# The last stage of an FNet and GEGLU kernel: two row tiles move from plain products into the seven-product scheme, and SiLU is taken per row tile

## The chip, the cores and the metric

The kernel runs on one core of a Trainium2 chip. The metric is the device time of one execution in microseconds; the time before is 771.11 us, the median of three runs (770.98 to 771.66). One further execution was taken by the hardware profiler; all durations of single instructions come from it.

## The reference

The input x has 2048 rows of 448 features, float32. What is computed:

```
xn = layernorm(x)
a, b = xn @ dft_hid_re.T, xn @ dft_hid_im.T          # DFT over the features
s    = dft_seq_re @ a - dft_seq_im @ b               # real part of the DFT over the rows
g    = silu((gelu(xn @ w_gate) * (xn @ w_up)) @ w_down)
out  = x + s * g
```

The two DFTs over the rows are products of a 2048x2048 and a 2048x448 matrix each. They are the last stage, and the change is in it.

## The kernel before

Every float32 operand is split into a high part of reduced precision, which TensorE takes in one pass, and a low part (the rest). A product is then high by high, and high by low, and low by high.

The stages follow each other: layernorm and transposes of x; gate, up and down of the GEGLU, with g summed into a DRAM tensor `gs`; the **hidden stage**, which computes a and b for 16 row tiles k of 128 rows (`hid_mm`, 22 products each); and the **last stage**, about 285 us long, which this case is about.

In the last stage the 16 output row tiles are done in eight pairs. For a pair j the sum over k runs over 16 **units**. For 14 row tiles k a unit is the function `seven`: a Strassen-like scheme with seven products in place of eight, each two matmuls (128x448 and 128x224), into seven PSUM banks that gather over the units. For the two row tiles in `KP` (10 and 15) a unit, called t0 and t1, is the function `plain`: twelve matmuls of 128x448 for one output row tile, into a bank of its own.

Each unit needs coefficients. `load_c` brings raw columns of the DFT matrix (`ct`, 192 KB, on SP's queue) and sums that were made earlier in DRAM (`sums`, 128 KB, on POOL's queue) into one of five raw buffers; a plain unit needs `cp` alone (256 KB). `sum_c` adds two more sums on VectorE (lines 1051 and 1052). `prep_c` splits the raw buffer: the high part on ScalarE (line 142), the low part on VectorE (line 143), into one of four slots that go round, and then asks for the load of five units on into the raw buffer just read. While TensorE works on unit m, the program's order has VectorE do `sum_c(m + 4)` and then `prep_c(m + 3)`. A slot is free for the high part of unit m + 3 when TensorE is done with unit m - 1.

The split values of a row tile k, seven blocks of 448 columns, lie in SBUF (`TS`). There isn't room for all: two tiles of the set `KX` are in SBUF at a time, the other two in DRAM (`td`), and each pair loads two of them on ScalarE's queue (line 1287, four loads for each tile, at the units named in `LOAD_AT`). The order of the row tiles alternates, so that a pair begins with the tiles with which the last one ended.

At a pair's end `gather` adds the seven banks into the two output tiles: one copy on ScalarE (line 1247) and seven operations of VectorE (lines 1249 to 1255). After that come one addition for each tile's halves, the addition of the plain bank (1309, 1316), the product with g (1262), the addition of x by a DMA (1264) and the store; five of these VectorE operations are handed out one to a unit in the next pair. SiLU of g was taken in the hidden stage, on four chunks of 1792 columns, read from `gs` and written back (line 1101). The last pair has an order of its own (`last_pair`).

The order on every engine is written out by hand: the program's text is the order of each engine's queue, and semaphores carry the waits between them.

Of the kernel before, what the change touches and what calls it, by code (L numbers as in the profile page):

```python
# [45 lines left out]
def fnet_geglu(ctx: ExitStack, tc: tile.TileContext, x, ca, ct, cp, et, wgu, wd, out):  # L46
# [496 lines left out]
    with tc.manual_schedule():  # L543
# [231 lines left out]
        sums = [dram.tile([P, NS, 2 * P], F32, name=f"sums{j}") for j in range(NK // 2)]  # L775

        def sum_step(at):


            for d in (0, 2):  # L780
# [3 lines left out]
                for n in (slice(0, NS // 2), slice(NS // 2, NS)):  # L784
# [124 lines left out]

        td = {k: dram.tile([P, 7 * D], F32, name=f"td{k}") for k in KX[0] + KX[1]}  # L910
        new = {}

        def place(tag, n):
# [11 lines left out]
            4: lambda: vt[1],  # L925
            5: lambda: slot(1),
            6: lambda: slot(0),
            7: lambda: a_x[1],
            8: lambda: a_h[0],
            9: lambda: a_h[1],  # L930
            11: lambda: a_x[2],
            12: lambda: place("st", 8 * D),
            13: lambda: place("x0", 4096),
            14: lambda: a_x[3],
        }
# [10 lines left out]
        def f_at(k):  # L946
            return (a_t if k % 2 == 0 or k > 12 else a_r[0])[:, : 8 * HD]

        TS, ab, ab_at, behind = {}, {}, {}, []
# [19 lines left out]
        def hid_plain(k, ps, spots):  # L969
            ab_at[k] = spots  # L970
# [6 lines left out]
            ab[k] = [(v[:, :D], v[:, D:]) for v in spots]  # L977
# [19 lines left out]
        def hid_split(k):  # L997

            f = fs[k].rearrange("p (i d) -> p i d", d=HD)[:, :7]
            TS[k] = AT[k]()[:, :T7]  # L1000
# [12 lines left out]
        units = [(j, k) for j in range(NK // 2) for k in order(j) + ["t0", "t1"]]  # L1013
        UN = NS + 2

        def raw_at(m):
            if m in (4, 5, 9, 10):
                return cc[:, 896 * ((m + 1) % 5) :][:, :896]
            i = (2, 0, 1, 2, 0, 0, 0, 1, 2)[m] if m < 9 else (m - 11) % 5
# [3 lines left out]
        nxt = {0: 3, 1: 6, 2: 7, 3: 8, 9: None, 10: None}  # L1023
# [9 lines left out]
        def load_c(m):  # L1033
# [7 lines left out]
            if isinstance(k, str):  # L1041
                nc.sync.dma_start(v[:, : 4 * P], cp[2 * j + int(k[1])])
            else:
                nc.sync.dma_start(v[:, : 3 * P], ct[j, :, KS.index(k)])
                nc.gpsimd.dma_start(v[:, 4 * P : 6 * P], sums[j][:, KS.index(k)])  # L1045
# [22 lines left out]
        g_in = {}  # L1068
        for k in [*range(14), 15, 14]:
# [6 lines left out]
            if k == 13:  # L1076
                behind.pop(0)()
# [8 lines left out]
            if k not in KP:  # L1086
                behind.append(lambda k=k: hid_split(k)())
                if k == 13:
                    behind.pop()()
# [3 lines left out]
            if k == 4:  # L1093
                x0 = sb.tile([P, 4096], F32, name="g_in", tag="x0")
            for c, at, v in ((2, 3, (a_st, 0)), (3, 4, None), (0, 4, None), (1, 5, (a_st, 1))):
                if k == at:
                    v, i = v or (x0, int(c == 0))
                    g_in[c] = part(v, 4 * D * i, 4, D)
                    nc.sync.dma_start(g_in[c], gv[:, 4 * c : 4 * c + 4])
                if k == at + 3:  # L1100
                    nc.scalar.activation(g_in[c], g_in[c], AF.Silu)
                    nc.sync.dma_start(gv[:, 4 * c : 4 * c + 4], g_in[c])
# [6 lines left out]
            if k == 12:  # L1109
                load_c(1)  # L1110
                load_c(2)
            if k == 13:
                sum_c(3)
        cc = sb.tile([P, 4 * D], F32, name="cc", tag="d1")
        load_c(4)
        load_c(5)
# [7 lines left out]
        gx = [v[:, o : o + D].bitcast(F32) for v, o in ((E_IN[2], 4 * D), (new["st"], T7))]  # L1124
# [12 lines left out]
        LOAD_AT = 2, 3, 4, 5, 6, 7, 8, 9  # L1137
        LAST_AT = 2, 2, 3, 4, 5, 6, 7, 8
# [6 lines left out]

        def seven(m, ps, n=1, only=None):

            for q, (i, b) in PRODUCTS.items():
                if only and q not in only:
                    continue  # L1150
                for u in range(m, m + n):
                    v = TS[units[u][1]][:, b * D : (b + 1) * D]
# [6 lines left out]
                        start=False, stop=u % UN == NS - 1, skip_group_check=True,  # L1159
                    )  # L1160

        def plain(m, py):
            h, l = c_hl.pop(m)
            for i, k in enumerate(KP):
                for r in range(2):
                    vh, vl = ab[k][r]
                    o = (2 * i + r) * P
                    a, b = h[:, o : o + P], l[:, o : o + P]
                    nc.tensor.matmul(py[:, :D], a, vh, start=i + r == 0, stop=False)  # L1169
                    nc.tensor.matmul(py[:, :D], a, vl, start=False, stop=False)  # L1170
# [219 lines left out]
```

## Time and profile before

| quantity | value |
|---|---|
| median of three runs | 771.11 us |
| time of the profiled execution | 771.12 us |
| span of the profiled execution, first to last instruction | 769.0 us |
| TensorE busy / VectorE / ScalarE / GpSimd | 99% / 71% / 48% / 23% |
| granted TensorE clock | 1.00 |
| DMA moved | 170.04 MB, mean 221 GB/s |

PE is TensorE's matmul, PEld its weight load, DVE VectorE, ACT ScalarE, POOL GpSimd and SP the sync engine, which only issues DMAs. A matmul's duration is longer than the distance to the next one's start, since matmuls are pipelined; the distance is what counts. So it is with VectorE: an operation on 128x896 is shown with 1.08 us, and the next begins 1.00 us after its start. The DMA share can exceed 1 where packets overlap.

### The profile page before, as it was taken

What the parts mean: (1) busy time and instruction counts of PE and PEld (TensorE: products, weight loads), DVE (VectorE), ACT (ScalarE), POOL (GpSimd) and SP (SyncE); (2) the same over time, 40 slices, a digit from 0 to 9 for tenths busy, and PEclk for the clock granted to TensorE, in tenths of its full rate; (3) what the DMA queues carried; (4) which work ended last, traced back from release to release, by engine and by line L of the source; (5) the groups of instructions that cost most, each with busy time, mean ns of one, the idle gap of its engine ahead of it and who ended that gap; (6) DMA issues with size and microseconds to landing.
All of it is one profiled execution on the core that took longest, in us unless ns stands there. A gap on an engine that the chain in (4) does not pass through costs nothing.

```text
span 769.0 us, 11358 instructions
## 1 busy us (share of the span) xinstructions
PE 763.1 (99%) x4056; PEld 687.5 (89%) x4056; DVE 544.8 (71%) x948; ACT 365.4 (48%) x545; POOL 177.5 (23%) x300
## 2 busy tenths in 40 slices
PE   9999999999999999999999999999999999999997
PEld 8988888888888888888889999999999999999997
DVE  7889877555556556455452776888888797979787
ACT  4875554444444344344444585544444444434341
POOL 1204033330511511501011001223232222313130
PEclk9999999999999999999999999999999999999999
DMA  8234458994959968774989981959696969788794
GB/s 295 92 119 145 150 202 171 263 185 102 264 111 248 272 116 227 169 158 84 258 217 242 370 343 55 315 177 340 203 355 205 349 206 334 219 295 266 255 310 155
DMA packets 61369, 170.04 MB, mean 221 GB/s; under 512 B 7424, under 2 KB 40064, under 8 KB 60416
## 3 DMA queue, kind: packets, MB, share of 16 engines
q0 software_dynamic: 13728, 61.02, 34.9%
q1 hardware_dynamic: 34128, 82.48, 30.5%
q10 hardware_dynamic: 13456, 25.81, 9.2%
q8 instruction: 32, 0.52, 0.3%
q14 instruction: 25, 0.20, 0.1%
HBM read 127.21 MB, written 70.91 MB: 258 GB/s over the span
## 4 chain that ended last, share of the span: by engine, by line
PE 96%; DVE 3%; ACT 1%; issue 0%; DVEq 0%; ACTq 0%
PE x L465 24%; PE p L1154 22%; PE po L442 18%; PE p L1157 10%; PE ab L965 9%; PE x L472 4%; PE gu L388 3%; PE py L1169 1%; PE py L1171 1%; PE py L1170 1%; PE warm L565 1%; DVE st L155 1%; PE p L1187 0%; PE pt L198 0%; DVE xt L215 0%; DVE xr_a L189 0%
## 5 line engine op out<-in xcount | busy, mean ns | idle before, releaser
L465 PE MATMUL x<-xt,w 128*128 128x512 f32 x480 | 149.5, 392 | 0.0
L465 PEld LDWEIGHTS x<-xt,w 128*128 128x128 f32 x480 | 90.1, 188 | 16.4 <-DVE tmp L504 0.7
L449 ACT ACTIVATE po_out<-po 128x448 f32<-128x448 f32 x112 | 60.1, 537 | 81.6 <-PE po L442 79.2
L442 PE MATMUL po<-wd0h,hs 128*128 128x448 f32 x256 | 81.7, 366 | 0.1
L454 POOL DMA_DIRECT2D gs<-po_out x24 | 21.4, 890 | 218.8 <-ACT po_out L449 213.6
L965 PE MATMUL ab<-e,xt 128*128 128x448 f32 x288 | 68.8, 365 | 0.0
L442 PE MATMUL po<-wd,hs 128*128 128x448 f32 x288 | 66.0, 365 | 0.0
L465 PE MATMUL x<-t_v,w 128*128 128x512 f32 x216 | 60.7, 389 | 0.0
L442 PEld LDWEIGHTS po<-wd,hs 128*128 128x128 f32 x288 | 54.1, 188 | 6.7
L965 PEld LDWEIGHTS ab<-e,xt 128*128 128x128 f32 x288 | 54.1, 188 | 4.3
L442 PEld LDWEIGHTS po<-wd0h,hs 128*128 128x128 f32 x256 | 48.1, 188 | 5.2 <-DVE tmp L416 0.3
L465 PEld LDWEIGHTS x<-t_v,w 128*128 128x128 f32 x216 | 40.5, 188 | 8.7
L1045 POOL DMA_DIRECT2D raw<-sums x45 | 24.8, 551 | 96.5 <-DVE xt L143 58.5
L442 PE MATMUL po<-wd0l,hs 128*128 128x448 f32 x128 | 46.9, 366 | 0.0
L142 ACT ACTIVATE e<-raw 128x896 fp32r<-128x896 f32 (+1 forms) x30 | 27.7, 922 | 39.0 <-DVE raw L1052 26.1
L520 ACT ACTIVATE hs<-tmp 128x512 fp32r<-128x512 f32 x24 | 15.2, 634 | 54.5 <-DVE tmp L518 54.5
L465 PE MATMUL x<-t_lo,w 128*128 128x512 f32 x96 | 37.4, 389 | 0.0
L142 ACT ACTIVATE e<-tmp 128x896 fp32r<-128x896 f32 (+1 forms) x22 | 19.7, 897 | 36.3 <-DVE tmp L1052 26.8
L1154 PE MATMUL p<-t_v,wd0l 128*128 128x448 f32 x112 | 36.4, 374 | 0.0
L1154 PE MATMUL p<-w,e 128*128 128x448 f32 x112 | 36.4, 374 | 0.0
L1045 POOL DMA_DIRECT2D tmp<-sums x39 | 21.4, 550 | 61.1 <-DVE xt L143 44.5
L350 DVE TENSOR_TENSOR w<-raw,w 128x512 fp32r<-128x512 f32 (+1 forms) x24 | 21.3, 888 | 18.3 <-ACT w L348 18.3
(369 smaller groups left out, 2016.8 us busy)
## 6 DMA issues: line engine op xcount, KB each, us to landing
gs<-po_out POOLq DMA_DIRECT2D x24, 896.0 KB, 8.5
sums<-ca SPq DMA_DIRECT2D x16, 896.0 KB, 10.0
sums<-ca POOLq DMA_DIRECT2D x16, 896.0 KB, 14.6
t_v<-td ACTq DMA_DIRECT2D x24, 448.0 KB, 5.8
w<-td ACTq DMA_DIRECT2D x24, 448.0 KB, 7.3
raw<-ct SPq DMA_DIRECT2D x45, 192.0 KB, 4.2
raw<-wgu SPq DMA_DIRECT2D x12, 640.0 KB, 5.9
tmp<-ct SPq DMA_DIRECT2D x39, 192.0 KB, 4.6
```

The lines of the kernel that those rows point to most:

```text
L142: nc.scalar.activation(h, src, AF.Copy)
L350: nc.vector.tensor_sub(w[:, 1408 + lo : 1408 + b], raw[:, P + lo : P + b], hw[:, lo:b].bitcast(F32))
L388: nc.tensor.matmul(ps[:, cols], a, xt[:, cols], start=n == 0, stop=n == len(mm) - 1)
L442: nc.tensor.matmul(po[:, :D], hs[:, a, kk * P : (kk + 1) * P], wdn[b][:, i], start=n == 0, stop=n == 5,)
L449: nc.scalar.activation(out_[0][:, kk], po[:, :D], AF.Copy)
L454: nc.gpsimd.dma_start(gv[:, 4 * c : 4 * c + 4], out_[0], accum_op=ALU.add)
L465: nc.tensor.matmul(ps, a[i], b[j], start=first and n == 0, stop=n == 2, skip_group_check=True)
L472: nc.tensor.matmul(ps, a[0], xt, start=False, stop=True, skip_group_check=True)
L965: nc.tensor.matmul(p[:, :D], a, b, start=n == 0, stop=n == len(mm) - 1)
L1045: nc.gpsimd.dma_start(v[:, 4 * P : 6 * P], sums[j][:, KS.index(k)])
L1154: nc.tensor.matmul(ps[q][:, :D], h, v, start=u % UN == 0, stop=False, skip_group_check=True)
L1157: nc.tensor.matmul(ps[q][:, :HD], l, v[:, :HD], start=False, stop=u % UN == NS - 1, skip_group_check=True,)
```

## The change

All 16 row tiles go through `seven` in the first seven pairs; the plain units t0 and t1 are left to the last pair alone, whose plain row tiles are now 8 and 10. The set `KX` has three tiles on each side, so that six lie in DRAM and each pair loads three, in twelve loads at the units 1 to 11. The last two units of a pair are done together: for each product, the matmuls of both units, then the next product. So the banks are complete one after another, while the pair still runs, and `gather` follows at that place. The banks go round by one, so that the next pair begins on the one bank that is not waited for. The values of row tile 13 lie in four pieces (`wide`), in what was the room of the plain tiles.

SiLU on the four chunks is gone from the hidden stage, with its loads and stores. In its place ScalarE takes SiLU of one 128x448 tile after each tile's first addition (`sum_` in `give`), in place in the half of `cc` that this addition has just read, and the product with g reads it there.

```diff
-KR = (2, 3, 6, 7, 8, 9, 11, 12, 13, 14)
-KX = ((4, 5), (0, 1))
-KP = (10, 15)
-KS = sorted(KR + KX[0] + KX[1])
-NS = len(KS)
+KR = (3, 4, 6, 7, 9, 11, 12, 13, 15, 14)
+KX = ((5, 8, 10), (0, 1, 2))
+KP = KX[0][1:]
+KW = 13
+LAST = NK // 2 - 1
+NL = NK - len(KP)
 def order(j):
-    return [*KX[j % 2], *KR, *KX[(j + 1) % 2]]
+    k = [*KX[j % 2], *KR, *KX[(j + 1) % 2]]
+    return k if j < LAST else k[:NL] + ["t0", "t1"]
...
-        sums = [dram.tile([P, NS, 2 * P], F32, name=f"sums{j}") for j in range(NK // 2)]
+        sums = [dram.tile([P, NK, 2 * P], F32, name=f"sums{j}") for j in range(NK // 2)]
...
+        pd = {k: dram.tile([P, 4 * D], F32, name=f"pd{k}") for k in KP}
...
-            if k in KP:
-                hid_plain(k, ps, [rest(v) for v in ((vt[0], t_lo[0]), (place("x0", 4096), a_x[2]) if k > 10 else None)[k > 10]])
-            else:
-                hid_sums(k, ps)()
+            hid_sums(k, ps)()
+            if k in KP:
+                hid_plain(k, ps)
...
-                if k == at + 3:
-                    nc.scalar.activation(g_in[c], g_in[c], AF.Silu)
-                    nc.sync.dma_start(gv[:, 4 * c : 4 * c + 4], g_in[c])
+            if k == 5:
+                nc.scalar.activation(tbl, epst, AF.Silu)
...
-        LOAD_AT = 2, 3, 4, 5, 6, 7, 8, 9
-        LAST_AT = 2, 2, 3, 4, 5, 6, 7, 8
+        LOAD_AT = 1, 2, 3, 4, 5, 5, 6, 7, 8, 9, 10, 11
+        LAST_AT = 1, 2, 3, 4, 5, 5, 6, 7
...
         def give(j, t):
             c = cs[t][0]
             def out_():
-                nc.vector.tensor_mul(c, c, gx[t])
+                nc.vector.tensor_mul(c, c, cs[t][1])
                 nc.gpsimd.dma_start(c, xv[:, 2 * j + t, :D], accum_op=ALU.add)
                 stores.append(lambda: nc.sync.dma_start(ov[:, 2 * j + t], c))
-            return [lambda: nc.vector.tensor_add(c, c, cs[t][1]), out_]
+            def sum_():
+                nc.vector.tensor_add(c, c, cs[t][1])
+                nc.scalar.activation(cs[t][1], gx[t], AF.Silu)
+            return [sum_, out_]
...
+            if u < (NL - 2 if j == LAST else UN - 2):
+                seven(m, ps)
+            elif j < LAST and u == UN - 2:
+                seven(m, ps, 2)
...
+            if m:
                 sum_c(m + 4)
                 prep_c(m + 3)
+            if u == UN - 2:
+                todo = gather(ps)
+                for f in todo[:6]:
+                    f()
+            if u == UN - 1:
+                todo[6]()
+                spare = give(j, 0) + give(j, 1)
+                banks = banks[7:] + banks[:7]
+                continue
+            if m == 2:
+                behind.pop()()
...
+                sums14()
             if m == 6:
                 hid_split(14)()
```

The change moves instructions on VectorE at the pair's end. Before, there stand in a row, from the first of the seven gathering operations of the second pair (`p_1` are its banks, `cc` the output tiles; `xt_67` and `wd0l`, then `e_3019`, `e_2921` are the slots of the units):

```order
L1249 TENSOR_TENSOR cc<-cc,p_1_4179 128x2x224
L1250 TENSOR_TENSOR cc<-cc,p_1_4180 128x2x224
L1251 TENSOR_TENSOR cc<-cc,p_1_4181 128x2x224
L1051 TENSOR_TENSOR raw_d_3414<-raw_d_3414 128x128
L1052 TENSOR_TENSOR raw_d_3414<-raw_d_3414 128x128
L143 TENSOR_TENSOR xt_67<-raw_74,wd0l 128x896
L1252 TENSOR_TENSOR cc<-cc,p_1_4182 128x2x224
L1253 TENSOR_TENSOR cc<-p_1_4182,cc 128x2x224
L1254 TENSOR_TENSOR cc<-cc,p_1_4183 128x2x224
L1255 TENSOR_TENSOR cc<-p_1_4184,cc 128x2x224
L1309 TENSOR_TENSOR cc<-cc,py_1_4481 128x448
L1051 TENSOR_TENSOR tmp<-tmp 128x128
```

And now, at the same place of the changed program:

```order
L1263 TENSOR_TENSOR cc<-cc,p_1_4209 128x2x224
L1264 TENSOR_TENSOR cc<-cc,p_1_4210 128x2x224
L1265 TENSOR_TENSOR cc<-cc,p_1_4211 128x2x224
L1266 TENSOR_TENSOR cc<-cc,p_1_4212 128x2x224
L1267 TENSOR_TENSOR cc<-p_1_4212,cc 128x2x224
L1268 TENSOR_TENSOR cc<-cc,p_1_4213 128x2x224
L1082 TENSOR_TENSOR tmp<-tmp 128x128
L1083 TENSOR_TENSOR tmp<-tmp 128x128
L145 TENSOR_TENSOR e_2921<-tmp,e_2921 128x896
L1269 TENSOR_TENSOR cc<-p_1_4214,cc 128x2x224
L1082 TENSOR_TENSOR raw_74<-raw_74 128x128
L1083 TENSOR_TENSOR raw_74<-raw_74 128x128
```

Six of the seven now stand together, ahead of the sums and the low part of the third unit to come, and the addition of a plain bank is gone.

On ScalarE, before, from the copy of the first bank of the same pair on (`td` are the kept tiles' loads):

```order
L1247 ACTIVATE cc<-p_1_4178 128x2x224
L142 ACTIVATE wd0l<-raw_74 128x896
L142 ACTIVATE e_3019<-raw_d_3414 128x896
L142 ACTIVATE e_2921<-tmp 128x896
L142 ACTIVATE t_v_820<-tmp 128x896
L142 ACTIVATE wd0l<-raw_74 128x896
L1287 DMA t_v_820<-td_3214 128x2x448
L142 ACTIVATE e_3019<-raw_74 128x896
L1287 DMA t_v_820<-td_3214 128x896
```

And in the changed program:

```order
L1261 ACTIVATE cc<-p_1_4208 128x2x224
L144 ACTIVATE e_2921<-tmp 128x896
L144 ACTIVATE t_v_820<-tmp 128x896
L1284 ACTIVATE cc<-e_3019 128x448
L1299 DMA t_v_820<-td_3215 128x2x448
L144 ACTIVATE wd0l<-raw_74 128x896
L1299 DMA t_v_820<-td_3215 128x896
L144 ACTIVATE e_3019<-raw_74 128x896
L1284 ACTIVATE cc<-ts_st 128x448
L1299 DMA t_v_820<-td_3215 128x2x448
```

The rows of line 1284 are SiLU. Each stands ahead of a high part and of a kept tile's load, and behind it in the queue wait the high parts of all later units.

More of the change, by code (lines that the diff above doesn't have):

```diff
@@ L999, in hid_split, with low @@
             f = fs[k].rearrange("p (i d) -> p i d", d=HD)[:, :7]
+            if k == KW:
+                for i, v in enumerate((vt[0], t_lo[0], place("x0", 4096), a_x[2])):
+                    w = min(2, 7 - 2 * i)
+                    wide.append(rest(v))
+                    v = wide[i][:, : w * D].rearrange("p (i w d) -> p i w d", i=w, w=2)
+                    nc.scalar.activation(v[:, :, 0], f[:, 2 * i : 2 * i + w], AF.Copy)
+                def low():
+                    for i in range(4):
+                        w = min(2, 7 - 2 * i)
+                        v = wide[i][:, : w * D].rearrange("p (i w d) -> p i w d", i=w, w=2)
+                        nc.vector.tensor_sub(v[:, :, 1], f[:, 2 * i : 2 * i + w], v[:, :, 0])
+                return low
             TS[k] = AT[k]()[:, :T7]
@@ L1122, in fnet_geglu @@
         sum_c(4)
[L1124 removed]
+        gx = [E_IN[2][:, 4 * D : 5 * D].bitcast(F32)]
         cv = [
@@ L1158, in seven @@
                         ps[q][:, :HD], l, v[:, :HD],
-                        start=False, stop=u % UN == NS - 1, skip_group_check=True,
+                        start=False, stop=u % UN == UN - 1, skip_group_check=True,
                     )
[L1162 to L1170, printed above, removed]
-                    nc.tensor.matmul(py[:, :D], b, vh, start=False, stop=i + r == 2)
         def plain_half(m, t, p, s, wide):
@@ L1209, in last_pair @@
             plain_half(m + 3, 1, py, 1, False)
+            gz = [raw_at(m + 7)[:, t * D : (t + 1) * D] for t in range(2)]
+            for t in (1, 0):
+                nc.scalar.activation(gz[t], gx[t], AF.Silu)
             x_ = [raw_at(m + 4 + t)[:, :D] for t in range(2)]
@@ L1334 @@
+            if m == 6:
+                hid_split(14)()
+            if spare:
+                spare.pop(0)()
+            if u in STORE_AT and stores:
+                stores.pop(0)()
 def kernel(A_x, A_dft_seq_re, A_dft_seq_im, A_dft_hid_re, A_dft_hid_im, B_x, B_w_gate, B_w_up, B_w_down):
```

169 lines of the change are left out of this document (72 added, 97 removed).

## The prediction

> **What bounds the kernel now.** I read the page first: the engines' shares, then the chain of work that ended last.
>
> ```profile
> span 769.0 us, 11358 instructions
> PE 763.1 (99%) x4056; PEld 687.5 (89%) x4056; DVE 544.8 (71%) x948; ACT 365.4 (48%) x545; POOL 177.5 (23%) x300
> PE 96%; DVE 3%; ACT 1%; issue 0%; DVEq 0%; ACTq 0%
> ```
>
> TensorE never rests, so the time is the number of matmuls by their distance, as long as the others stay ahead. How far ahead they are decides this case, so next come the stretches of the last stage: us, busy time of TensorE, weight loads, VectorE, ScalarE and GpSimd with their counts, granted clock, DMA share, GB/s. The first row is one whole pair, the others one pair in stretches of two units, and the start of the next.
>
> ```profile
> 546.00:581.60 35.60, 35.60 (x222) 33.85 (x221) 29.83 (x58) 15.07 (x17) 9.50 (x16) 1.00 0.82 273
> 586.60:591.00 4.40, 4.40 (x30) 4.20 (x29) 4.29 (x9) 2.57 (x3) 1.09 (x2) 1.00 0.41 120
> 591.00:595.40 4.40, 4.40 (x30) 4.20 (x29) 4.33 (x10) 2.18 (x3) 2.01 (x3) 1.00 0.93 280
> 595.40:599.80 4.40, 4.40 (x30) 4.20 (x29) 4.33 (x9) 1.94 (x3) 1.11 (x2) 1.00 1.02 303
> 599.80:604.20 4.40, 4.40 (x30) 4.20 (x29) 2.80 (x7) 1.04 (x2) 2.01 (x3) 1.00 1.05 376
> 604.20:608.60 4.40, 4.40 (x30) 4.20 (x29) 3.55 (x7) 2.78 (x3) 0.00 (x0) 1.00 1.06 352
> 608.60:613.00 4.40, 4.40 (x29) 4.20 (x29) 3.37 (x5) 1.63 (x3) 1.99 (x4) 1.00 1.06 400
> 613.00:617.10 4.10, 4.10 (x27) 3.90 (x27) 1.94 (x5) 1.98 (x3) 0.73 (x2) 1.00 0.88 274
> 617.10:622.10 5.00, 5.00 (x27) 4.64 (x26) 4.97 (x10) 0.96 (x1) 0.55 (x1) 1.00 0.36 115
> ```
>
> VectorE is full for the first 13 us of a pair and again at its end; between, it rests. The DMA engines are full from 591 to 613, while the kept tiles come in. TensorE waits for neither. In the timeline of VectorE (start, duration, line, and in brackets what it waited for) the distance between them can be read:
>
> ```profile
> 596.29 1.08 DVE L143 TENSOR_TENSOR e<-tmp,e 128x896 fp32r<-128x896 f32 x1
> 597.29 0.62 DVE L1268 TENSOR_TENSOR cc<-cc 128x448 f32<-128x448 f32 x1
> 597.83 0.28 DVE L1051 TENSOR_TENSOR raw<-raw 128x128 f32<-128x128 f32 x1
> 598.36 1.08 DVE L143 TENSOR_TENSOR xt<-tmp,t_v 128x896 fp32r<-128x896 f32 x1
> 603.04 0.29 DVE L1051 TENSOR_TENSOR raw_d<-raw_d 128x128 f32<-128x128 f32 x1 [1.53 <-DMA raw_d<-ct]
> 603.58 1.09 DVE L143 TENSOR_TENSOR e<-raw,e 128x896 fp32r<-128x896 f32 x1
> 614.31 0.69 DVE L143 TENSOR_TENSOR xt<-raw_d,t_v 128x512 fp32r<-128x512 f32 x1
> 616.24 0.62 DVE L1249 TENSOR_TENSOR cc<-cc,p 128x448 f32<-128x448 f32 x1 [1.25 <-PE p L1157]
> ```
>
> From start to start: a low part takes 1.00 us, the two sums of a unit 0.53, a 448-wide operation 0.53. So a unit costs VectorE 1.53.
>
> **What TensorE saves.** TensorE's timeline, two matmuls seven units apart, and the first matmul of the plain unit t0, with its first and last start over seven pairs:
>
> ```profile
> 561.89 0.37 PE L1154 MATMUL p<-xt,e 128*128 128x448 f32 x1
> 577.24 0.38 PE L1154 MATMUL p<-t_v,wd0l 128*128 128x448 f32 x1
> L1169 PE MATMUL py<-t_v,e x7: 375/375/375, 510.5 to 723.9; 128*128 128x448 f32 x7
> ```
>
> A unit is (577.24 - 561.89) / 7 = 2.193 us. A pair is (723.9 - 510.5) / 6 = 35.57, so t0 and t1 take 35.57 - 14 x 2.193 = 4.87. Two units of seven products take 4.39. Saved: 0.48 a pair, **3.4 us** over seven pairs. The last pair and the hidden stage keep their matmuls.
>
> **What is hidden in the hidden stage.** Removed: four SiLU of 1.70 us and four loads and stores of 896 KB. Added: the splits of two more row tiles (on VectorE four sums and a low part each, 3 us; on ScalarE 2.3) and stores of two kept tiles and two plain ones.
>
> ```profile
> 442.83 1.70 ACT L1101 ACTIVATE po_out<-po_out 128x1792 f32<-128x1792 f32 x1
> 417.20:480.00 62.80, 62.80 (x312) 58.21 (x311) 42.07 (x67) 39.62 (x46) 5.04 (x9) 1.00 0.71 265
> sums<-ca SPq DMA_DIRECT2D x16, 896.0 KB, 10.0
> ```
>
> VectorE has 20 us free here and ScalarE 23, and TensorE's matmuls cover both: nothing. (Uncovered, it would be 6 us.) The sums made earlier grow from 14 to 16 row tiles, 128 KB more on each of 32 DMAs in a stage whose queues TensorE doesn't wait for: nothing. Row tile 13's split in four pieces and row tile 15's split stand right where the last stage begins. There VectorE has 3 us more to do in the first seven units; I take **+0.2** (bounds 0, and 0.8 if all lead is gone there).
>
> **What the pair's end costs.** Here I count from the moment when TensorE starts the double unit (units 14 and 15, 4.39 us). In the best case VectorE is as far ahead as the slots allow. Then: low part of the next pair's unit 1 done at 1.9, six gathering operations to 5.1 (TensorE completes a bank each 0.63 us, and the next pair needs the sixth at 6.3: no wait), unit 2 at 6.65, the seventh at 7.2, unit 3 at 8.7, first addition 9.25. Now ScalarE's order matters: SiLU waits for that addition, and the high part of unit 4 waits behind SiLU. From the rows
>
> ```profile
> 590.34 0.95 ACT L142 ACTIVATE wd0l<-raw 128x896 fp32r<-128x896 f32 x1 [0.58 <-DVE raw L1052]
> L1247 ACT ACTIVATE cc<-p x8: 527/544/544, 508.8 to 756.1; 128x448 f32<-128x448 f32 x8
> ```
>
> (the copy of line 1247 has SiLU's shape) it is 9.25 + 0.54 + 0.95 + 1.0 = 11.75 for the low part of unit 4, where VectorE alone would be done at 10.8. TensorE needs it at 4.39 + 4 x 2.193 = 13.16. The second SiLU does the same to unit 6: done at 16.75, needed at 17.55. **The lead is 0.8 us at unit 6**, and then VectorE regains 2.193 - 1.53 = 0.66 a unit. So with all loads in time nothing stalls, but VectorE may come to the pair's end no more than 0.8 late.
>
> Does it? Before, the plain units gave it rest: one low part of 512 columns each, no sums. The rows at 614.31 and 616.24 show it done with t1 by 615.0, 4.6 us before TensorE needs it, then waiting for TensorE. That rest is gone, and so is the rest of the DMA queues: kept tiles come from unit 1 to unit 11 in place of 2 to 9. Coefficients, issue to landing, while kept tiles stream (three pairs), and when they don't:
>
> ```profile
> raw<-ct SPq DMA_DIRECT2D x2, 192.0 KB, 6.2
> tmp<-ct SPq DMA_DIRECT2D x2, 192.0 KB, 7.1
> raw<-ct SPq DMA_DIRECT2D x2, 192.0 KB, 6.8
> raw_d<-ct SPq DMA_DIRECT2D x1, 192.0 KB, 4.0
> w<-td ACTq DMA_DIRECT2D x3, 448.0 KB, 7.5
> td<-t_v POOLq DMA_DIRECT2D x2, 1568.0 KB, 8.6
> raw_d<-ct SPq DMA_DIRECT2D x1, 192.0 KB, 7.6
> raw_d<-ct SPq DMA_DIRECT2D x1, 192.0 KB, 5.6
> ```
>
> (The last two are single loads: the one behind the wait at 603.04, and one of the first pair.)
>
> A raw buffer's round: low part of unit p done, load of unit p + 5 (L), its sums (0.53), low part of unit p + 4 (1.0). That is four units in L + 0.1 + 1.53, and TensorE takes 8.77 for four. At L = 4 VectorE goes as fast as it can; at L = 6.5 it regains only 0.16 a unit; from L = 7.1 on it loses. The wait of 1.53 at 603.04 is this.
>
> With L = 6.5 from unit 5 on, I follow the loads: sums of units 10 to 13 are held to 20.4, 23.3, 25.5 and 27.0, and the low part of unit 15 is done at 35.1, where the double unit needs it at 35.4; a full lead would have it at 32.6. VectorE then starts the gathering 1.1 late: over 0.8, so 0.3 of stall at unit 6. With L = 7.0 unit 15's is done at 36.1: 0.7 of stall at the double unit, and 0.4 to 0.8 at unit 6, since the next pair starts with less. Bounds of a pair's end: 0 (L up to 6.0) and 2.0 (L = 7.3). The rows lie at 6.2 to 7.1, and the stream lasts longer than before; I take 0.9 for six ends (pairs 1 to 6, the last one's start counted with them) and 0.2 after pair 0, whose units carry no outputs: **+5.6**.
>
> **The sum**, against the profiled execution's 771.12 us (span 769.0 and 2.1 around it; the median of the runs is 771.11, the same): -3.4 + 0.2 + 5.6 = +2.4, so **773.5 us**.
>
> **The rivals.** *Clean*: the loads come within 6 us, as the 5.6 of the first pair, where kept tiles stream beside coefficients and no outputs; stalls stay under 0.2 in all, 771.1 - 3.4 = **767.7**. For it: TensorE waits nowhere in the last stage now, and VectorE's work in a pair, 16 x 1.53 + 11 x 0.53 = 30.3, is under 35.1. Against: 7 us in the rows above. It decides below L = 6.2. *Half*: stalls of 0.3 to 0.7 an end use up what the matmuls give: 769.6 to 772.6, at L = 6.3 to 6.6. *The DMA engines become the bound*:
>
> ```profile
> DMA packets 5484, 9.72 MB, mean 273 GB/s; under 512 B 695, under 2 KB 4520, under 8 KB 5480
> ```
>
> A pair now moves 9.72 MB and 1568 KB for a third tile, 640 KB of coefficients less 512 KB of `cp`: 11.46 MB. Some 6.5 us around its end carry coefficients only (320 KB in 2.193 us, 1.0 MB); the other 10.5 at 342 GB/s, the mean of the five full stretches, take 30.7: 37.2 against 35.1, six pairs by 2.1, **780**. Against: the last full stretch moved 400 GB/s. The Trainium skill, "DMA: Bandwidth & Descriptors", section "Specifications", gives an HBM limit of about 358 GB/s for a core; by that rate, an estimate, a pair would be 35.7 us and the kernel 771. The row of 400 GB/s does not agree, and the measurement decides: 358 is no ceiling here. That the change doesn't do what it says is excluded by the order of its instructions.
>
> **How the numbers follow.** Late loads with stalls of 0.7 and more, 0.40; clean, 0.30; half, 0.22; DMA bound, 0.08. The likeliest gives 773.5, its own range 771.5 to 779. Clean lies inside the whole range, as does the DMA bound: 767.5 to 780. About 0.2% (1.5 us) is what a measurement of this kernel can tell from no change. Faster by more: clean and a little of half, 0.32; within: most of half and the low end of late loads, 0.23; slower: 0.45.
>
> **What would show it.** Right: waits of TensorE's weight loads for the low part (now line 145) in each pair from the third on, at unit 6 and at the double unit, 0.5 to 1.5 us a pair; VectorE waiting for `ct` in units 8 to 15; seven matmul stretches of 35.09 us without these. Wrong, to the good side: no such waits, pairs of 35.1 us. Wrong, to the bad side: TensorE waiting for `td`, or a DMA share of 1 through the whole pair. Wrong in the start: a stall of over 1 us in the first seven units. If the coefficients' landing stays at 6 us though kept tiles stream for 11 units, my step from the stream's length to L is the one that failed.

## The result, and the profile after

The changed kernel takes **804.01 us** (median of 4 runs, 801.15 to 806.16) against 771.05 (770.41 to 771.66): 1.0427 times the time before, 95% interval 1.0414 to 1.0440. It is slower by 33 us. The forecast was 773.5, with 780 as the upper end: the sign was right, the size wrong by a factor of fourteen.

The page of the changed kernel: span, TensorE's share, and the shares of the chain that ended last, by engine.

```profile
span 804.4 us, 11570 instructions
PE 775.0 (96%) x4084; PEld 687.2 (85%) x4084; DVE 556.7 (69%) x975; ACT 376.2 (47%) x567; POOL 187.9 (23%) x318
PE 62%; DVE 16%; DMA 14%; issue 4%; ACT 3%; DVEq 0%; SPq 0%; ACTq 0%
```

Before, TensorE's part of the chain was 96% and no transfer stood in it. Now VectorE has 16% and transfers have 14%.

Where in the program? The copy with which ScalarE begins a pair's gathering marks the pairs. Its row, with first and last start (eight pairs):

```profile
L1261 ACT ACTIVATE cc<-p x8: 523/527/546, 515.4 to 791.5; 128x448 f32<-128x448 f32 x8
```

From the first copy to the seventh, the stretches of the profile (us, busy TensorE, weight loads, VectorE, ScalarE, GpSimd with counts, granted clock, DMA share, GB/s):

```profile
515.40:757.98 242.58, 223.96 (x1353) 202.93 (x1352) 184.43 (x355) 99.34 (x115) 63.90 (x108) 1.00 0.87 285
595.56:635.64 40.08, 36.96 (x224) 33.16 (x223) 30.75 (x60) 16.58 (x21) 10.65 (x18) 1.00 0.86 283
```

Six pairs take 242.58, so one takes 40.43. TensorE's own work is 35.09, as the prediction had it. **Each pair loses 5.34 us**, six lose 32.0. The DMA engines aren't full over the pair (0.87), and VectorE rests for 9 of its 40 us.

TensorE loses more in the first pair. Its first matmul starts at 479.09 (479.50 before). The first matmul of unit 11, after and before:

```profile
507.79 0.37 PE L1176 MATMUL p<-ts_st,t_v 128*128 128x448 f32 x1
```

```profile
503.90 0.38 PE L1154 MATMUL p<-xt,t_v 128*128 128x448 f32 x1
```

That is **3.9 us late**. The account of the profiled execution (span 804.4 against 769.0, 35.4): -3.4 for TensorE's matmuls, +3.9 in the first pair, +32.0 in six pairs, and as the remainder 2.9 behind the seventh copy.

Who makes TensorE wait? The waits of the whole changed kernel (engine and line, who released it: us in total, times, longest):

```profile
ACT cc L1284 <- DVE cc L1283: 37.2, 14, 2.9
DVE raw L1082 <- DMA raw<-ct: 17.5, 14, 2.8
DVE tmp L1082 <- DMA tmp<-ct: 16.7, 11, 4.2
PEld p L1179 <- DVE e L145: 15.0, 18, 2.7
PEld p L1179 <- DVE xt L145: 11.1, 13, 2.2
PEld p L1176 <- issue: 5.5, 6, 1.0
PE p L1176 <- DVE cc L1267: 4.1, 6, 0.8
```

Three steps of one chain: ScalarE stands for SiLU (line 1284) till VectorE's addition is done, VectorE stands for coefficients, and TensorE stands for VectorE. It does so at two places. Its weight loads wait for low parts (line 1179, 26.1 us in all). And at a pair's start they wait 11.0 us for the banks, which VectorE's late gathering (lines 1263 to 1268) hasn't yet emptied; the row with "issue" is the weight load ahead of the matmul that waits for line 1267. The second pair's ScalarE, with its transfers (rows marked ACTq, line 1299, are issues of kept tiles' loads), shows what SiLU holds up:

```profile
564.14 0.58 ACT L1284 ACTIVATE cc<-e 128x448 f32<-128x448 f32 x1 [2.52 <-DVE cc L1283]
564.14 0.38 ACTq L1299 DMA_DIRECT2D t_v<-td  x1
564.72 0.33 ACTq L1299 DMA_DIRECT2D t_v<-td  x1
...
569.41 0.58 ACT L1284 ACTIVATE cc<-ts_st 128x448 f32<-128x448 f32 x1 [2.92 <-DVE cc L1283]
569.42 0.38 ACTq L1299 DMA_DIRECT2D t_v<-td  x1
...
569.94 0.47 ACTq L1299 DMA_DIRECT2D t_v<-td  x1
570.64 0.59 ACTq L1299 DMA_DIRECT2D w<-td  x1
...
571.27 0.53 ACTq L1299 DMA_DIRECT2D w<-td  x1
```

Six of the twelve loads leave in two bursts behind the two SiLU, four of them within 2 us. What follows on VectorE, 9 us behind the second burst:

```profile
580.02 0.29 DVE L1082 TENSOR_TENSOR raw_d<-raw_d 128x128 f32<-128x128 f32 x1 [2.90 <-DMA raw_d<-ct]
```

This raised three suspects: SiLU's place on ScalarE, the third kept tile, and what is new in the first pair.

### The profile page after: what moved, and what is told of

The parts are those of the page before. It is cut to its first block, busy times and chain, and to the rows that moved or that the text cites. A ratio compares the mean times of both kernels' runs of the same rounds, so it can differ in the third digit from the quotient of the medians.

```text
span 804.4 us, 11570 instructions
## 1 busy us (share of the span) xinstructions
PE 775.0 (96%) x4084; PEld 687.2 (85%) x4084; DVE 556.7 (69%) x975; ACT 376.2 (47%) x567; POOL 187.9 (23%) x318
## 4 chain that ended last, share of the span: by engine, by line
PE 62%; DVE 16%; DMA 14%; issue 4%; ACT 3%; DVEq 0%; SPq 0%; ACTq 0%
PE x L467 23%; PE po L444 17%; PE ab L976 9%; DMA tmp<-ct 4%; PE x L474 4%; PE p L1176 4%; DMA raw<-ct 4%; DMA raw_d<-ct 4%; DVE e L145 3%; DVE xt L145 3%; PE gu L390 2%; PE p L1179 2%; DMA w<-td 1%; ACT wd0l L144 1%; DVE cc L1283 1%
## 5 line engine op out<-in xcount | busy, mean ns | idle before, releaser
L1176 PE MATMUL p<-w,e 128*128 128x448 f32 x161 | 55.1, 379 | 0.0
L1076 POOL DMA_DIRECT2D raw<-sums x50 | 27.6, 552 | 90.5 <-DVE e L145 42.3
L1076 POOL DMA_DIRECT2D tmp<-sums x48 | 26.4, 551 | 92.1 <-DVE e L145 45.8
L1179 PE MATMUL p<-w,e 128*128 128x224 f32 x161 | 43.0, 267 | 0.0
L1176 PE MATMUL p<-t_v,e 128*128 128x448 f32 x128 | 42.5, 375 | 0.0
L1179 PE MATMUL p<-t_v,e 128*128 128x224 f32 x128 | 34.8, 272 | 5.5 <-DVE e L145 5.5
```

The lines of the kernel that those rows point to most:

```text
L1076: nc.gpsimd.dma_start(v[:, 4 * P : 6 * P], sums[j][:, k])
L1176: nc.tensor.matmul(ps[q][:, :D], h, v, start=u % UN == 0, stop=False, skip_group_check=True)
L1179: nc.tensor.matmul(ps[q][:, :HD], l, v[:, :HD], start=False, stop=u % UN == UN - 1, skip_group_check=True,)
```

## The experiments

Times are medians; "a pair" is the mean distance of the first to the seventh gathering copy by sixths, from ScalarE's timeline, and what it has over TensorE's 35.09 (35.57 where the plain units are still there) stands behind it.

| kernel | us | a pair | over |
|---|---|---|---|
| before | 771.1 | 35.57 | 0 |
| the change | 804.0 | 40.43 | 5.34 |
| SiLU a unit later | 786.8 | 37.35 | 2.26 |
| no loads of the third kept tile | 789.0 | 37.58 | 2.49 |
| both of these | 773.8 | 35.41 | 0.32 |
| before, SiLU per row tile | 775.5 | 36.16 | 0.59 |

### One at a time: SiLU's place, the third tile

```diff
+            def silu_():
+                nc.scalar.activation(cs[t][1], gx[t], AF.Silu)
-            return [sum_, out_]          # SiLU inside sum_
+            return [sum_, silu_, out_]   # one a unit, behind its high part
```

> The changed kernel, but each SiLU of the last stage stands one unit later on ScalarE, behind that unit's high part: the addition that it reads is then long done, ScalarE doesn't wait, and the kept tiles' loads behind it leave on time. VectorE's seventh unit-filling step moves back by two units, nothing else changes. Theory A (ScalarE held by SiLU bunches the loads of the kept tiles and holds high parts): most of the 31 us goes, 772 to 780. Theory B (the volume of the third kept tile and the full set of coefficients makes coefficients late, wherever SiLU stands): at least 795. Half of each: 783 to 792.

Measured: 786.84 us (1.0207, interval 1.0177 to 1.0236). This lies between the two theories: a good half of the 33 us is gone. Of TensorE's weight loads' waits in six pairs 10.6 us are now for the banks at a pair's start, and 3.3 for low parts:

```profile
PEld p L1176 <- issue: 6.1, 6, 1.0
PE p L1176 <- DVE cc L1267: 4.7, 6, 0.8
PEld p L1179 <- DVE xt L145: 2.9, 5, 1.0
```

```diff
-            nc.scalar.dma_start(a.bitcast(F32), b)
+            if i < 2 or j == LAST:
+                nc.scalar.dma_start(a.bitcast(F32), b)
```

> The changed kernel, but the loads of the third kept tile are left out in all pairs but the last (9 to 11 MB less; the output is then not the reference's). SiLU stays where it is. Theory A: the bunch behind SiLU stays (it is made of the first and second tiles' loads), 790 to 800. Theory B: 768 to 776, since the volume of a pair is then that of the kernel before.

Measured: 789.04 us, between the two theories again: nearly half of the 33 us is gone.

> Both edits: SiLU a unit later and the third kept tile's loads left out in all pairs but the last (the output is then not the reference's). If A and B together are the whole cause, 767 to 769 (TensorE's own work: 771.1 less 3.4). If the missing rest of VectorE at a pair's end (the plain units are gone) costs something by itself, 771 to 778.

Measured: 773.75 us (771.65 to 775.16). A pair of this kernel, beside one with SiLU later alone and one with the third tile alone left out (a stretch of each; columns as above):

```profile
585.55:620.65 35.10, 35.10 (x226) 33.51 (x226) 30.72 (x60) 16.89 (x21) 10.90 (x19) 1.00 0.87 285
```

```profile
590.62:628.27 37.65, 36.73 (x230) 33.98 (x229) 30.81 (x60) 16.86 (x20) 10.63 (x18) 1.00 0.92 309
```

```profile
628.35:665.93 37.58, 36.72 (x229) 34.02 (x228) 30.63 (x60) 16.54 (x20) 10.60 (x18) 1.00 0.81 263
```

With both edits TensorE works through this pair: 35.10, as in four of the six; two pairs lose 0.9, which makes the mean of 0.32. Over that 0.32 the third tile alone costs 1.94 a pair, SiLU's place alone 2.17, and both together 5.02: 0.9 more than their sum, so each makes the other dearer. The time lies in the range that was to speak for the plain units' missing rest of VectorE, but most of what it has over 767 to 769 is the first pair's. That rest by itself costs at most 0.3 a pair.

> The kernel before with only one part of the change: SiLU of g is taken per row tile in the last stage, right behind the addition, and the four SiLU of the hidden stage with their loads and stores are left out. Theory A (SiLU in ScalarE's queue does it by itself): 780 to 800. Theory B, and also a cause that needs both: 771 to 774.

Measured: 775.49 us (1.0056, interval 1.0030 to 1.0082). Slower, though not by the amount expected: 0.59 a pair, where SiLU's place costs 2.2 to 3.1 in the changed kernel. That the plain units cover part of it is likely, but not tested by itself. The counterpart, with SiLU a unit later in the kernel before:

> The kernel before with SiLU per row tile, one unit behind the addition that frees its place (ScalarE doesn't wait for it), and without the hidden stage's SiLU, loads and stores. If the SiLU's own time (0.58 us, twice a pair) costs nothing and only its wait did (775.5 with it right behind the addition): 770.5 to 772. If its place on ScalarE costs anyway: 773 to 775.

Measured: 770.40 us, ratio 0.9997 (0.9985 to 1.0008): no difference. Two SiLU a pair on ScalarE cost nothing measurable; the wait does.

### What of the third tile costs: bytes, number or place

```diff
+            if i == 2 and j < LAST:
+                a, b = a[:, :1, :64], b[:, :1, :64]
             nc.scalar.dma_start(a.bitcast(F32), b)
```

> SiLU a unit later, and the four loads of the third kept tile stay in all pairs but the last, but each brings only 128 x 64 numbers (32 KB in place of 224 or 448 KB; the output is then not the reference's). The number of transfers and what waits for their issue stay, the volume of a pair falls from 11.46 to 10.0 MB. If the volume is what the third tile costs: 772 to 777, as without these loads (773.8). If it is their number (each transfer of SP and ScalarE takes one of eight completion semaphores in turn, and ScalarE stands still until the transfer eight before it has landed, 20 us in all in the run with SiLU later): 781 to 787.

Measured: 774.16 us, 35.43 a pair. All twelve transfers are there, and the cost is not: their number isn't the cause.

```diff
+            q = nc.gpsimd if i == 2 and j < LAST else nc.scalar
-            nc.scalar.dma_start(a.bitcast(F32), b)
+            q.dma_start(a.bitcast(F32), b)
```

> SiLU a unit later, and the four loads of the third kept tile are issued by GpSimd in place of ScalarE in all pairs but the last. Volume and times of issue are meant to stay; ScalarE no longer stands still for their issue, and they take turns with GpSimd's transfers. If the volume is the cause: 785 to 790. If the issue on ScalarE is: 772 to 778. GpSimd issues in order and waits there for the low parts that free its buffers; were that late, it would show as TensorE waiting for the kept tile.

Measured: 784.07 us (782.80 and 785.34), 36.94 a pair. The issue on ScalarE has about 0.4 of the 2.26, by one profile each. This wait of the kernel with SiLU later is gone here:

```profile
ACT e L144 <- DMA out<-cc: 20.2, 6, 4.0
```

(The releaser is an output's store: a load's issue waits till the transfer that had its completion semaphore before it has landed. The loads of this run wait on GpSimd instead, so their times aren't quite the same.)

```diff
-                nc.gpsimd.dma_start(v[:, 4 * P : 6 * P], sums[j][:, k])
+                if j < 1 or j == LAST:
+                    nc.gpsimd.dma_start(v[:, 4 * P : 6 * P], sums[j][:, k])
```

> SiLU a unit later, all three kept tiles loaded, but the loads of the sums (128 KB a unit, GpSimd's queue) left out in pairs 1 to 6: 9.4 MB a pair, under the kernel before's 9.7, with the kept tiles' stream as long as in the change (the output is not the reference's). If it is the sum of the bytes that costs 2.3 us a pair: pairs of 35.1 to 35.6, 772 to 775. If it is that kept tiles stream from unit 1 to 11 beside the coefficients: 37 a pair, 783 to 787.

Measured: 772.68 us, 35.49 a pair. Here the kept tiles' stream is as long and as large as in the change, and other bytes are missing. So the stream's length alone is not the cause; the result fits the sum of the bytes. (VectorE no longer waits for the sums either, but with SiLU later these waits were 3.5 us in six pairs, and 11.2 us are won.) The DMA parts of the page for one pair of the kernel with SiLU later, of this one, and of the one without the third tile (packets, MB, mean GB/s):

```profile
DMA packets 6549, 11.65 MB, mean 309 GB/s; under 512 B 816, under 2 KB 5647, under 8 KB 6546
```

```profile
DMA packets 5508, 9.13 MB, mean 261 GB/s; under 512 B 525, under 2 KB 5121, under 8 KB 5505
```

```profile
DMA packets 5664, 10.01 MB, mean 285 GB/s; under 512 B 751, under 2 KB 4869, under 8 KB 5660
```

At 10.0 MB a pair, with the loads spread out, TensorE is fed; at 11.6 it isn't. The coefficients' landing shows why. Of two pieces of the changed kernel's second pair (573 to 577 and 585 to 589) the rows are:

```profile
tmp<-ct SPq DMA_DIRECT2D x2, 192.0 KB, 8.2
tmp<-ct SPq DMA_DIRECT2D x2, 192.0 KB, 7.5
```

By such rows, as means over four pairs, landings of over 6 us last from about 15 to 33 us behind a gathering copy in the changed kernel, and to 31 us with SiLU later. Without the third tile, and without the sums, they rise to 8 us as well, but end at about 24 us, and VectorE catches up. So what the bytes add is not a later single landing, but more units with late ones.

Does the volume cost as much in the kernel before, with its plain units?

```diff
+            if u in (4, 6, 8, 10) and j < NK // 2 - 1:
+                ...   # a kept tile's part, from DRAM to a DRAM tile of its own
+                nc.scalar.dma_start(more, b)
```

> The kernel before, and in each pair but the last four more transfers on ScalarE's queue in units 4, 6, 8 and 10, of the size of one kept tile (1568 KB, from DRAM to DRAM, which nothing reads). The DMA engines then have 11.3 MB and more a pair. If the volume costs 2 us a pair wherever it is added: 780 to 788. If the plain units' rest of VectorE covered it: 770.5 to 774.

Measured: 789.40 us, 38.32 a pair, 2.75 over. The added transfers cost as much here, but by another way. ScalarE stands 17.5 us for issues, in four waits, ahead of a unit's high part, and TensorE waits for that high part and for the low part behind it:

```profile
ACT t_v L142 <- DMA w<-td: 17.5, 4, 4.7
PEld p L1154 <- ACT t_v L142: 6.0, 6, 1.6
PEld p L1157 <- DVE xt L143: 5.6, 6, 0.9
```

These 11.6 us are most of the 16.5 that six pairs lose; in two of the pairs the clock halves behind the stop as well. So the plain units don't cover it, but this run doesn't part the bytes from the wait of the issue.

### What SiLU's wait does

> The changed kernel with SiLU in its place, and all twelve loads of kept tiles issued by GpSimd in all pairs but the last. This parts what SiLU's wait on ScalarE does: if it is that it bunches the loads, the pairs fall from 40.2 to about 37.5 us and the kernel to 785 to 790; if it is the late high parts of units 4 and 6, the loads' queue changes little: 798 to 804.

Measured: 815.11 us, 41.69 a pair: worse, and neither answer. The loads wait now on GpSimd ahead of the sums, and VectorE waits for the sums, which in the changed kernel it hardly does:

```profile
DVE tmp L1082 <- DMA tmp<-sums: 17.8, 16, 3.0
DVE raw L1082 <- DMA raw<-sums: 17.0, 17, 2.4
```

So another test:

```diff
-            nc.scalar.dma_start(a.bitcast(F32), b)
+            if j == LAST:
+                nc.scalar.dma_start(a.bitcast(F32), b)
```

> The changed kernel with SiLU in its place, and without any load of kept tiles in all pairs but the last (6.8 MB a pair; the output is then not the reference's). With SiLU in its place and two tiles loaded, a pair took 37.6 us, 2.5 over TensorE's work. If SiLU's wait costs by bunching these loads, pairs of 35.1 to 35.5 and a kernel of 772 to 775. If it costs by holding the high parts of units 4 and 6 while VectorE has no lead, loads or not: 36.5 to 37.6 a pair, 780 to 789.

Measured: 773.90 us, 35.18 a pair. SiLU waits as long as in the change, its row and a pair's:

```profile
ACT cc L1284 <- DVE cc L1283: 38.0, 14, 2.9
```

```profile
585.79:620.96 35.17, 35.17 (x226) 33.51 (x226) 30.59 (x59) 16.42 (x21) 10.62 (x18) 1.00 0.65 187
```

TensorE loses no more than 0.1 a pair. With coefficients in time (6.7 MB a pair), that is what the held high parts alone cost. The margin is thin, though. Unit 6 of the next pair, its low part on VectorE and TensorE's first matmul with it:

```profile
601.36 1.09 DVE L145 TENSOR_TENSOR e<-tmp,e 128x896 fp32r<-128x896 f32 x1 [0.95 <-ACT e L144]
```

```profile
602.54 0.34 PE L1179 MATMUL p<-xt,e 128*128 128x224 f32 x1
```

The low part is done 0.1 us before it is needed. What else stands behind SiLU is the loads. The next run has SiLU a unit later, no third tile, and the eight other loads at about the times that SiLU's wait gave them:

```diff
-        LOAD_AT = 1, 2, 3, 4, 5, 5, 6, 7, 8, 9, 10, 11
+        LOAD_AT = 2, 2, 5, 5, 5, 6, 7, 8, 8, 9, 10, 11
```

> SiLU a unit later and the third kept tile's loads left out (as in the run of 773.8 us, pairs of 35.4), but the eight loads that stay are issued in units 2, 2, 5, 5, 5, 6, 7, 8 in place of 1, 2, 3, 4, 5, 5, 6, 7: about the times at which they left when SiLU stood in its place (9.3, 9.8, 14.5 to 16.1, 18.4, 21.7 us behind the gathering's copy; pairs of 37.6). If SiLU's wait costs through the late and bunched loads: pairs of 36.8 to 37.6, 781 to 787. If it needs the held high parts as well: pairs under 36, 772 to 777. The output is not the reference's.

Measured: 783.77 us, 37.12 a pair, against 35.41 with the loads spread. SiLU waits 0.5 us at most here, and 1.7 of the 2.2 us that its wait costs (37.58 against 35.41) are there: later and bunched loads can do most of it. The 1.7 may be a little too much, since the last two loads left 2 to 3 us later than SiLU's wait had made them. For the other 0.5 nothing was tried.

### The first pair

The changed kernel's VectorE (start, duration, line) between the low parts of units 5 and 6:

```profile
487.95 1.08 DVE L145 TENSOR_TENSOR e<-po_out,e 128x896 fp32r<-128x896 f32 x1
490.62 1.79 DVE L1036 TENSOR_TENSOR ts_st<-tmp,ts_st 128x1568 fp32r<-128x1568 f32 x1 [1.58 <-ACT ts_st L1033]
492.33 0.38 DVE L1007 TENSOR_TENSOR cc<-cc 128x224 f32<-128x224 f32 x1
...
494.19 1.08 DVE L145 TENSOR_TENSOR e<-raw,e 128x896 fp32r<-128x896 f32 x1
```

Row tile 15's split goes into the buffer in which units 4 and 5 have their coefficients, so its high part can begin only when unit 5's low part is done. VectorE waits 1.58 for it, then makes its low part (1.7) and the four sums of row tile 14 (1.3). TensorE meanwhile:

```profile
495.33 0.37 PE L1179 MATMUL p<-xt,e 128*128 128x224 f32 x1 [2.41 <-DVE e L145]
```

Three moves of this work, the first two with SiLU a unit later, the third with the third tile left out as well:

```diff
             if m == 2:
                 behind.pop()()          # first: the low part a unit later; third: made by GpSimd
-                sums14()
-            if m == 6:
+            if m == 5:
+                sums14()                # all three
+            if m == 7:
                 hid_split(14)()
```

> SiLU a unit later, and in the first pair the low part of row tile 15's split stands a unit later, behind the sums for unit 7, the sums of row tile 14 three units later and its split one unit later. In the runs so far TensorE stands 2.7 us still at 495.3 in the first pair, behind VectorE's 1.6 us wait for the high part of tile 15 and 3 us of work for these tiles. If that is the cause, the first pair's gathering starts 1.3 to 2 us sooner (at 513.9 to 514.6 in place of 515.9) and the kernel takes 784.8 to 785.6; if the first coefficients' loads are, nothing moves: 786.8.

> SiLU a unit later, and of the first pair's work only the sums of row tile 14 moved three units later (1.3 us of VectorE) and its split one unit later; the split of row tile 15 and the loads of units 9 and 10 stay. TensorE's stop of 2.4 us at 495.3 should shrink by 1.3, and the first gathering begin at 514.5 in place of 515.9; the kernel 785 to 786.

> SiLU a unit later and the third kept tile's loads left out in all pairs but the last (773.8 us so far; the output is then not the reference's). In the first pair the low part of row tile 15's split is made by GpSimd in place of VectorE, the sums of row tile 14 stand three units later and its split one. If the 2.4 us stop at 495.3 comes from the 4.6 us that these put ahead of unit 6's low part in VectorE's queue: it is gone, the first gathering begins at 511.2 to 512.2 in place of 514.5, and the kernel takes 770 to 772. If it comes from the first coefficients' landing: over 513, 772 to 774.

Measured: 786.54, 789.23 and 774.86 us; the first gatherings at 515.98, 515.63 and 516.08. With only the sums moved, by 1.33 us, the stop shrinks by 1.33, from 2.41 to 1.08, and with the low part moved too, to 0.56:

```profile
494.28 0.37 PE L1179 MATMUL p<-xt,e 128*128 128x224 f32 x1 [1.08 <-DVE e L145]
```

```profile
493.29 0.37 PE L1179 MATMUL p<-xt,e 128*128 128x224 f32 x1 [0.56 <-DVE e L145]
500.06 0.38 PE L1179 MATMUL p<-xt,xt 128*128 128x224 f32 x1 [2.11 <-DVE xt L145]
```

So the stop is this work's, microsecond for microsecond. But nothing is won; the gain that was forecast came in none of the three. In the first move unit 9's low part stops TensorE in place of unit 6's (the 2.11 above). The loads for units 9 and 10 leave at 492.3, no later than in the changed kernel (492.4). But two parts of a kept tile left at 490.0 and 490.4 in place of 494.4, and beside them the sums land in 6.2 us in place of 3.3. In the second move stops of 0.40 and 0.77 follow at units 9 and 11, behind the work that was moved there. In the third the low part of the split took 3.54 on GpSimd, and VectorE's low part of unit 6 beside it 3.70 in place of 1.08, so that a stop of 2.30 stayed; this run says nothing of the first coefficients' landing (two timelines of the third move, GpSimd's and VectorE's):

```profile
490.97 3.54 POOL L1036 TENSOR_TENSOR ts_st<-tmp,ts_st 128x1568 fp32r<-128x1568 f32 x1 [4.89 <-ACT ts_st L1033]
```

```profile
491.75 3.70 DVE L145 TENSOR_TENSOR e<-raw,e 128x896 fp32r<-128x896 f32 x1 [1.89 <-ACT e L144]
```

A further variant, which leaves out the low part of row tile 15's split altogether, has no measured time.

### A version with fewer bytes and the result intact

```diff
-                nc.sync.dma_start(v[:, : 3 * P], ct[j, :, k])
-                nc.gpsimd.dma_start(v[:, 4 * P : 6 * P], sums[j][:, k])
+                nc.sync.dma_start(v[:, : 4 * P], ct[j, :, k])
...
+                nc.gpsimd.tensor_add(b, cr2, cr1)
+                nc.gpsimd.tensor_add(cr2, cr2, ci2)
```

> A version that keeps all seven-product units and all three kept tiles, with SiLU a unit later, but moves fewer bytes: the sums are no longer made ahead and loaded (128 KB a unit); the fourth coefficient block is loaded with the three others (256 KB a unit in all in place of 320), and GpSimd makes two of the four sums (0.5 to 1.05 us each by its rows of 128x128 additions in the profile of before). A pair then moves 10.4 MB. If bytes are what costs 2.3 us a pair: pairs of 35.2 to 36, the kernel 772 to 777. If GpSimd's 1 to 2 us a unit make the coefficients late in place of the loads, or hold VectorE up: pairs of 37 and more, over 784.

Measured: 829.99 us (1.0770, interval 1.0752 to 1.0788), 42.60 a pair: the second branch. VectorE's additions take longer beside GpSimd's, and then wait for them:

```profile
L1091 DVE TENSOR_TENSOR tmp<-tmp 128x128 f32<-128x128 f32 x34 | 13.7, 403 | 14.6 <-POOL tmp L1084 14.6
```

That is 0.40 us for one addition in place of 0.29. No version was found that beats the kernel before. So whether fewer bytes alone would help with the result intact stays open.

## Why the prediction was wrong, point by point

**TensorE's saving, 3.4 us: right.** Pairs without stops take 35.10 and 35.17.

**The hidden stage, nothing: right.** The last stage's first matmul starts at 479.09 in place of 479.50, and the kernel before without its SiLU there, with SiLU late enough in the last stage, takes the same time (770.4).

**The start, +0.2 with a bound of 0.8: wrong, 3.9.** The prediction named a stall of over 1 us in the first seven units as what would show it wrong, and that is what came, at unit 6. I had counted the splits of row tiles 13 and 15 as 3 us of VectorE that its lead would take. I did not follow the buffer that row tile 15's split is written to, so the wait for ScalarE's high part behind unit 5's low part (1.58) was missed, and row tile 14's sums, now two units earlier, weren't in it. The stop put TensorE 2.7 us back, and 1.6 more came through the clock (below): unit 11 begins 28.7 us behind the first matmul, and 27.1 with the thin third tile, which has the same stop at full clock. The first matmul's earlier start gives 0.4 back.

**The pair's end, 0.9 each: the step that failed**, in two terms. It came to 5.34 a pair.

The first is SiLU on ScalarE. "With all loads in time nothing stalls" was nearly right, as the run without kept tiles shows (0.1 a pair, with SiLU waiting as long as ever). "The lead is 0.8 us at unit 6" was not: there it is 0.1. The six gathering operations take 3.6 us in place of the 3.2 that I had counted, and the low part ahead of them is 0.2 late. So there was no slack for anything that came late. And I followed only the high parts behind SiLU. The kept tiles' loads stand in the same queue. They left in two bursts, and bursts like these cost 1.7 us a pair when they were made without SiLU's wait. The changed order that stands ahead of the prediction has a load right behind each SiLU; I read it and priced its neighbours only.

The second is L, the coefficients' landing. I took it from the kernel before's rows (6.2 to 7.1), let it rise to 7.3 at most, and so bounded a pair's end at 2.0. A landing taken while 9.7 MB a pair move says little on 11.5: in the changed kernel the rows reach 7.5 and 8.2, and landings of over 6 last for some 18 us of a pair. With SiLU out of the way 2.26 a pair are left, 1.94 of them the third tile's. The step from the stream's length to L failed as well, for with the stream unchanged and 128 KB a unit less of other bytes 0.4 a pair are left.

The place of the waits was only half right. I had the sixth bank emptied 1.2 us before the next pair needs it and called it "no wait". VectorE comes to the pair's end later than that, and a third of the changed kernel's waits, and three quarters of those with SiLU later, are for the banks.

**The rival that came nearest: DMA engines.** It gave 37.2 us a pair; with SiLU later a pair takes 37.35. I gave it 0.08, since one stretch of 4.4 us had moved 400 GB/s. The mean of a whole pair with its idle stretches never came near that: 309 with SiLU later. That the number fits so well is in part luck. The engines' share is 0.92 in that pair and not 1, and TensorE doesn't wait for kept tiles, but for a VectorE that late coefficients have held up. The rivals were also kept apart as if only one could hold, while the bytes, SiLU and the start come on top of each other: 2.26, 3.1 (5.34 less 2.26) and, once, 3.9.

**What would show it**: the waits for low parts and VectorE's waits for `ct` came as told, and the waits for banks, which weren't foreseen; together they are 5 us a pair in place of 0.5 to 1.5. The signs named for the bad side, TensorE waiting for `td` and a DMA share of 1 through the whole pair, did not come (the share is 0.86 in the changed kernel's pair from 595.56).

## What to carry to other kernels

A row's landing time belongs to the load under which it was measured: when a change adds bytes, compare bytes per stretch with the mean rate of whole stretches, idle ends included, and not with the best one. When an instruction that waits is put into an engine's queue, list everything behind it, transfers first: what was hidden as arithmetic can still bunch the loads, and late loads come back as somebody else's wait. Follow the buffer of a moved step as well as its engine: here a split that shared a buffer with coefficients cost four microseconds, and moving its pieces only moved the stop.

## What the hardware showed unexpectedly

**A stop of 2.4 us halves TensorE's clock, mostly.** Behind the stop at 495.3 the changed kernel's matmuls ran at half the granted clock for 3.4 us (the column ahead of DMA's share; a second stretch is from the end of the sixth pair):

```profile
496.50:499.50 3.00, 3.00 (x13) 2.78 (x11) 2.93 (x7) 2.43 (x3) 1.10 (x2) 0.50 0.99 322
755.90:759.10 3.20, 3.20 (x13) 2.94 (x12) 2.69 (x6) 1.38 (x2) 0.80 (x2) 0.50 0.62 190
```

Ten profiles have the same stop, of 2.41 or 2.42 us. In eight the clock then stood at half for 3.4 us, from some moment between 494.9 and 497.0 on; in two (both edits; the thin third tile) it stayed at 1.00, and these two have the earliest first gatherings, 514.5 and 513.9 against 515.4 to 516.2. Shorter stops did it too: one of 1.91 at 755.2 ahead of the second row, and one of 2.11 in the first move of the start. In the changed kernel's pair from 595.56, with stops of 0.2 to 0.8 us, the clock stayed at 1.00. The Trainium skill, "TensorE: Matmul & The Clock Gate", section "Part 1: The HAM clock gate (the "warmup" mystery)", has the clock halved after an idle window of about 3.4 us that runs freely. The length of the slow stretch and the chance in it agree with that; a stop of 2.4 us, and even of 1.9, was enough here, less than the window.

**GpSimd's additions hold up VectorE's.** A subtraction that takes 1.08 us alone took 3.70, and an addition 0.40 us in place of 0.29: both above. The long subtraction ended 0.94 us behind GpSimd's (495.45 against 494.51), so by these times it hardly moved on while GpSimd's ran. The Trainium skill, "GPSIMD Engine Reference", section "1. Specifications", says that GpSimd shares its SBUF interfaces with VectorE, with contention for instructions with two SBUF inputs. These runs agree, and give the price.
